# Eight consecutive rows of wo per partition, heads re-sorted by 0/1 products, and another order of the tail in a two-problem decode attention

## The chip, the cores and the metric

The kernel runs on one core of a Trainium2 chip. The metric is the time of one execution in microseconds on the device. Three executions of the kernel before took 377.95, 378.59 and 376.51 us (median 377.95). A fourth was recorded by the hardware profiler.

The core has a matrix engine (PE: a weight load followed by a matmul that streams up to 512 columns), a vector engine (DVE), a scalar engine (ACT), GpSimd (POOL), and SP, which here only issues transfers. Matmuls write to PSUM, the engines read from it, and transfers go between HBM and SBUF by 16 DMA engines. The engines run side by side and wait for one another through semaphores.

## The reference

Two independent problems A and B of the same shape, each one decode step with a sliding window; the outputs stand side by side.

```python
B, Sq, D = 2, 1, 576
Hq, Hkv, Sk, Dh = 32, 16, 16384, 128
W = min(4096, max(256, Sk // 4))                     # 4096
q = (x @ wq).reshape(B, Sq, Hq, Dh)                  # transposed to b h q d
k = repeat(k_cache[:, :, Sk - W:, :], 2, axis=1)     # 2 query heads share a kv head
v = repeat(v_cache[:, :, Sk - W:, :], 2, axis=1)
p = softmax(einsum("bhqd,bhkd->bhqk", q, k) * Dh ** -0.5)
o = einsum("bhqk,bhkd->bhqd", p, v)
out = o.reshape(B, Sq, Hq * Dh) @ wo                 # wo: [4096, 576]
```

Everything is bf16. For each of 2 x 32 pairs (problem, kv head, batch) a K slab and a V slab of 4096 x 128 elements, 1 MiB each, are read once. With wq and wo this makes 153 MB.

## The kernel before

**Units.** A *pair* i (0 to 63) is one kv head of one batch of one problem: 32 in A, then 32 in B. Two pairs in a row (both batches of one kv head) are a *norm unit* k = 0 to 31. Eight pairs are a *group* G = 0 to 7; a group covers four kv heads, so eight query heads, and has its own softmax and its own slice of wo (8 x 128 rows of 576 elements).

**Steps.** The body is a loop over time steps t, each with four quarters q. In step t DVE transposes the K slab of pair t (four STREAM_TRANSPOSE, L679), PE computes the scores of pair t - 1 (eight matmuls, L700) into one PSUM bank per group, and PE multiplies the V slab of pair t - LAG with the softmax weights, LAG = 11. Work that belongs between these is hung into tables by (step, quarter): `pe_pre` and `da_pre` ahead of the quarter's work, `da_post` behind it. Every operation is recorded with the operations it needs, and each engine runs its own list in the order of recording, waiting on semaphores.

**Softmax of a group.** After the last scores of group G (step T = 8G + 8) DVE takes the maximum (`c_max`, L377, in `da_post`), PE turns it (L381), DVE negates and copies it (L391, L401), PE spreads it (L406), ACT takes the exponential (L427) and DVE transposes the weights into `pT` (L473) and gathers them into `pC` (L487). The sums go by L431, L441, L448 and L451 into `rsb` (L463), in step T + 2.

**Values, two forms.** `is_a(i)` says which form a pair takes; the last NB_TAIL = 7 pairs are not `is_a`.
- `is_a`: eight matmuls with the small weights `pC` stationary and 512 columns of V moving (L765) into an accumulator bank `ACC[i % 2]`; eviction to `acc_sb[i % 2]` by ACT for even i (L780) and by DVE for odd i (L783); then, one step later, four matmuls with the identity (L743) combine the parts into the bank `OT[k % 2]`. In a step the combination of the pair before stands directly ahead of the product of the pair at hand.
- otherwise: 32 matmuls with V stationary and 56 columns of `pT` moving (L723), eight in each quarter, straight into `OT[k % 2]`. The last V slab arrives in four transfers, one per quarter.

**Norm and projection.** In step tn_of(k) DVE multiplies a unit's output by `rsb` (`make_norm`, L555, result `oTn`: 128 positions of a head in the partitions, two heads, two batches), clears the `OT` bank again (L565), and one quarter later PE multiplies it with its two heads of wo (`make_proj`, four matmuls of 2 x 288, L582) and adds it to columns 128 to 415 of both `OT` banks. At the end of each problem `make_E` copies these to `out_sb` (L597, L600), and two transfers write it out.

**Transfers.** SP issues all loads in one list. `stream` alternates K of pair t and V of pair t - LAG; they share a ring of NR = 9 slabs, and a slab's transfer waits until the slab nine places before it has been read. The wq chunks and the wo slices stand in the list ahead of given K slabs; the wo slice of group G stands ahead of K of pair 8G + 6, has two buffers `wob[:, G % 2]`, and waits for the last projection of group G - 2 (`deps` in `issue_wo`). SP works strictly in order: what stands behind a waiting transfer waits too.

The wo slice is read so that partition d holds row d of each of its eight heads: 1024 runs of 576 elements, 1,152 bytes.

Of the kernel before, what the change touches and what calls it, by code (L numbers as in the profile page):

```python
# [6 lines left out]
BF16 = mybir.dt.bfloat16  # L7
ACTF = mybir.ActivationFunctionType
# [51 lines left out]
def build_kernel(nc, probs, out, cfg=None):  # L60
# [6 lines left out]
    LAG = cfg.get("LAG", 11)  # L67
    NPT = 3
    NS = cfg.get("NS", 56)
    NB_TAIL = cfg.get("NB_TAIL", 7)  # L70
    WQ_AT = cfg.get("WQ_AT", 13)
    QP_AT = cfg.get("QP_AT", 21)
    WO_LEAD = cfg.get("WO_LEAD", 5)
# [37 lines left out]
    def pair_info(i):  # L111
# [3 lines left out]
        b = il % Bb  # L115
        return P, g, b

    def tile_cols(j):
        return (j % 16) * 32 + 16 * (j // 16)

    es = ExitStack()
    with es:
# [25 lines left out]
        rs = sb("rs", [1, 16], FP32)  # L148
        rsb = sb("rsb", [128, NPT, 16], FP32)
        oTn = sb("oTn", [128, 2, 2, Bb], BF16)  # L150
        acc_sb = sb("acc_sb", [8, 2, 512], BF16)
        pC = sb("pC", [128, NPT, 2, 8, 32], BF16)
        out_sb = sb("out_sb", [Bb, NPROB, NOUT], BF16)
# [131 lines left out]
        def issue_wo(G):  # L285
            P = G // GPP
            Gl = G % GPP
            woP = probs[P][4]
            h0 = Gl * 8
            pc = G % 2  # L290
            deps = [proj[4 * (G - 2) + 3]] if G >= 2 else []

            def f(e):
                return e.dma_start(wob[:, pc, :, :],
                                   woP[h0 * 128:(h0 + 8) * 128, :].rearrange("(h d) n -> d h n", d=128)).then_inc(wo_sem[pc], 16)
            wo_dma[G] = dma_op("sp", wo_sem[pc], 1, f, deps, "wo%d" % G)

        def ensure_stream_until(s_needed):
# [73 lines left out]
        def c_max(G):  # L372
            x = G % 2
            deps = [Sop[(8 * G + 7, NQ - 1)]]
            if G >= 1:
                deps.append(chain[(G - 1, "Tm")])
            chain[(G, "max")] = S.add("dve", lambda e: e.tensor_reduce(m1[:], ST[x][:, :], AX.X, ALU.max),  # L377
                                      deps, "cmax_%d" % G)
# [168 lines left out]
        def make_norm(k):  # L547
            x = k % 2
            G = (2 * k) // 8
            gl = k % 4  # L550
            pr = G % NPT
            orr = k % 2

            def f(e):
                return e.tensor_tensor(oTn[:, orr, :, :].rearrange("d h b -> d b h"),  # L555
                                       OT[x][:, 0:64 * Bb].rearrange("d (b c) -> d b c", b=Bb, c=64)[:, :, 0:2],
                                       rsb[:, pr, gl * 2 * Bb:(gl + 1) * 2 * Bb].rearrange("d (b h) -> d b h", b=Bb, h=2),
                                       ALU.mult)
            deps = [PVop[(2 * k + 1, NQ - 1)], chain[(G, "rsb")], ot_last_pe[x]]
            if k >= 2:  # L560
                deps.append(proj[k - 2])
            op = S.add("dve", f, deps, "norm_%d" % k)
            norm_mul[k] = op
            if k + 2 < NK:
                ot_zero[k + 2] = S.add("dve", lambda e: e.memset(OT[x][:, 0:64 * Bb], 0.0), [op], "otz_%d" % (k + 2))  # L565
            else:
                ot_zero[k + 2] = op
            ot_last_da[x] = ot_zero[k + 2]

        def make_proj(k):  # L570
# [17 lines left out]
            ot_last_pe[0] = proj[k]  # L588
            ot_last_pe[1] = proj[k]

        def make_E(P, which, final):
            k_last = (P + 1) * KP - 1
            deps = [proj[k_last], ot_last_pe[which]]
            if which == 0:
                if not final:
                    deps.append(norm_mul[k_last + 1])
                op = S.add("dve", lambda e: e.tensor_copy(out_sb[:, P, 0:NH], OT[0][0:Bb, ACC0:ACC0 + NH]),  # L597
                           deps, "Elo_%d" % P)
# [14 lines left out]
        def at(tbl, t, q, fn):  # L613
            tbl.setdefault((t, q), []).append(fn)

        da_post = {}
        for G in range(NG):
            T = 8 * G + 8
            at(da_post, T, 3, lambda G=G: c_max(G))
            at(pe_pre, T + 1, 0, lambda G=G: c_tm(G))  # L620
            at(da_pre, T + 1, 0, lambda G=G: c_nm(G))
            at(pe_pre, T + 1, 2, lambda G=G: c_bias(G))
            at(da_pre, T + 1, 2, lambda G=G: (c_exp(G), c_tpx(G)))
            at(da_pre, T + 1, 3, lambda G=G: c_gather(G))
            at(pe_pre, T + 2, 0, lambda G=G: c_ts(G))
            at(da_pre, T + 2, 0, lambda G=G: c_rs(G))
            if G + 2 < NG:
                at(da_pre, T + 2, 0, lambda G=G: make_st_zero(G + 2))
            at(pe_pre, T + 2, 1, lambda G=G: c_rsbm(G))
            at(da_pre, T + 2, 1, lambda G=G: c_rsb(G))  # L630
            P, Gl = G // GPP, G % GPP
            at(pe_pre, 2 * Gl if P == 0 else QP_AT + 8 * GPP * (P - 1) + Gl, 2 if G > 0 else 0, lambda G=G: make_qproj(G))
            at(pe_pre, max(0, 8 * G - 3), 2 if G > 0 else 0, lambda G=G: make_qjob(G))
        def tn_of(k):
            return (2 * k + 1) + LAG + (2 if is_a(2 * k + 1) else 1)
        for k in range(NK):
            tn = tn_of(k)
            at(da_pre, tn, 0, lambda k=k: make_norm(k))
            at(pe_pre, tn, 1, lambda k=k: make_proj(k))
        for P in range(NPROB):  # L640
            final = (P == NPROB - 1)
            k_last = (P + 1) * KP - 1
            tp_ = tn_of(k_last)
            if final:
                at(da_pre, tp_, 2, lambda P=P: (make_E(P, 0, True), make_E(P, 1, True)))
            else:
                at(da_pre, tp_, 2, lambda P=P: make_E(P, 1, False))
                assert tn_of(k_last + 1) > tp_
                at(da_pre, tn_of(k_last + 1), 0.5, lambda P=P: make_E(P, 0, False))

        def make_late_zero():
# [6 lines left out]
            ot_last_da[0] = init_zero["OT0"]  # L658
            ot_last_da[1] = init_zero["OT1"]
        at(da_pre, 1, 0, make_late_zero)  # L660

        NT = NP + LAG + 3
        for t in range(NT):
            for q in range(NQ):
# [21 lines left out]
                if 0 <= i < NP:  # L686
                    G = group_of(i)
                    x = G % 2
                    c = i % NKT
                    pl = i % 8  # L690
                    zr = G % NZQ

                    def fS(e, x=x, c=c, pl=pl, zr=zr, q=q):
                        last = None
                        jh = q // 2
                        for p4 in (2 * (q % 2), 2 * (q % 2) + 1):
                            b32, par = p4 // 2, p4 % 2
                            b0 = xt[:, c, 2048 * jh + 64 * b32 + par:2048 * jh + 64 * b32 + par + 1]
                            mv = bass.AP(b0.tensor, b0.offset, [list(b0.ap[0]), [128, 16], [2, 32]])
                            last = e.matmul(ST[x][:, 0:512], zq[:, p4, zr, pl, 16 - 16 * jh:144 - 16 * jh], mv,  # L700
                                            start=False, stop=True, skip_group_check=True)
                        return last
                    jh_ = q // 2
                    deps = [EVop[(i, 2 * jh_)], EVop[(i, 2 * jh_ + 1)], qev[G], st_zero[G]]
                    Sop[(i, q)] = S.add("pe", fS, deps, "S_%d_%d" % (i, q))
                i = t - LAG
                if 0 <= i < NP and not is_a(i):
                    sV = slab_idx[("V", i)]
# [180 lines left out]
```

## Time and profile before

| | |
|---|---|
| median of three executions (range) | 377.95 us (376.51 to 378.59) |
| the profiled execution: its time, its span | 378.42 us, 376.6 us |
| PE busy, DVE busy, ACT busy | 296.3 us (79%), 211.7 us (56%), 36.9 us (10%) |
| bytes moved, mean rate over the span | 153.41 MB, 407 GB/s |
| DMA packets, of them under 2 KB | 28661, 10592 |
| mean granted PE clock | 0.964 of full speed |
| L700 scores, one matmul of 512 columns | 391 ns, x512 |
| L765 values, one matmul of 512 columns | 397 ns, x456 |
| L582 projection, one matmul of 288 columns | 285 ns, x128 |
| L783, L780 eviction (DVE, ACT) | 679 ns, 586 ns |

The span runs from the first to the last instruction; the profiled execution's own time is 1.8 us more. The duration of one matmul contains its way through the array, which neighbours share: eight L765 matmuls in a row take 1.83 us and not eight times 397 ns. "Idle before" an instruction is put down to what ended it. The chain that ended last goes back from the last instruction to whatever released each one; a line of it gives its start, its length and what ran. In the stretches, a line gives the stretch, its length, the busy time of PE, of the weight loads, of DVE, ACT and POOL (with counts), the granted PE clock, the DMA engines' share and GB/s.

### The profile page before, as it was taken

Reading aid. Unit: us, or ns where it says so; the run is one execution under the profiler, and the core shown is the slowest. Engines: PE = TensorE matmul, PEld = TensorE weight load, DVE = VectorE, ACT = ScalarE, POOL = GpSimd, SP = SyncE. Lnnn points to the kernel's source line nnn. Section 1 sums busy time; section 2 is a strip of 40 time slices with the busy share of each in tenths; the row PEclk is TensorE's granted clock in tenths of the full one; section 3 lists DMA queues with packets and bytes.
Section 4 is the critical chain, followed back from the end, with each engine's and each line's share of the span. In section 5 each row is a group of like instructions: output and inputs, shape, how many; then the busy total and the mean of one; then the engine's idle time right before and its main releaser. Section 6 shows DMA issues by size and latency. Waiting matters only on the chain.

```text
span 376.6 us, 4709 instructions
## 1 busy us (share of the span) xinstructions
PE 296.3 (79%) x1960; PEld 118.6 (31%) x1960; DVE 211.7 (56%) x429; ACT 36.9 (10%) x105; POOL 6.7 (2%) x22
## 2 busy tenths in 40 slices
PE   0397778375898989969897789868799689959786
PEld 0243223122334433313332233323333233313245
DVE  3196894235664567626864567636773467633311
ACT  1101101000101010100101010100101001000100
POOL 7000000000000000000000000000000000000000
PEclk9999989799999999989999899999999899998899
DMA  8999999999999999999999999999999999999991
GB/s 310 425 421 412 419 419 411 422 420 422 422 416 417 418 420 420 410 421 421 423 419 411 422 419 422 410 422 421 422 422 410 420 425 419 413 421 418 425 411 70
DMA packets 28661, 153.41 MB, mean 407 GB/s; under 512 B 2392, under 2 KB 10592, under 8 KB 11360
## 3 DMA queue, kind: packets, MB, share of 16 engines
q1 hardware_dynamic: 28632, 153.11, 98.9%
q8 instruction: 15, 0.25, 0.3%
q14 instruction: 6, 0.05, 0.0%
q10 hardware_dynamic: 8, 0.00, 0.0%
HBM read 153.10 MB, written 0.00 MB: 407 GB/s over the span
## 4 chain that ended last, share of the span: by engine, by line
DMA 44%; PE 33%; DVE 10%; SPq 9%; issue 1%; ACT 1%
DMA ring<-in_B_v_cache_dram 17%; DMA ring<-in_A_v_cache_dram 15%; PE acc L765 15%; PE st L700 11%; DMA ring<-in_A_k_cache_dram 8%; SPq L272 7%; DMA ring<-in_B_k_cache_dram 5%; DVE xt L679 4%; PE ot L582 3%; DVE acc_sb L783 2%; PE ot L723 2%; PE ot L743 1%; ACT pR L427 1%; DVE m L377 1%; DVE pT L473 1%
## 5 line engine op out<-in xcount | busy, mean ns | idle before, releaser
L679 DVE STREAM_TRANSPOSE xt<-ring 128x512 f32<-128x512 f32 x256 | 159.3, 673 | 66.0 <-DMA ring<-in_A_k_cache_dram 38.5
L765 PE MATMUL acc<-ring,pC 128*8 128x512 bf16 x456 | 114.7, 397 | 38.1 <-DMA ring<-in_A_v_cache_dram 22.9
L700 PE MATMUL st<-xt,zq 128*128 128x512 bf16 x512 | 134.7, 391 | 4.9 <-DVE xt L679 4.5
L700 PEld LDWEIGHTS st<-xt,zq 128*128 128x128 bf16 x512 | 42.7, 98 | 74.1 <-issue 28.5
L765 PEld LDWEIGHTS acc<-ring,pC 128*8 128x8 bf16 x456 | 36.0, 89 | 91.1 <-DMA ring<-in_A_v_cache_dram 24.5
L783 DVE CAST acc_sb<-acc 8x512 bf16<-8x512 f32 x28 | 19.0, 679 | 66.8 <-PE acc L765 66.8
L780 ACT ACTIVATE acc_sb<-acc 8x512 bf16<-8x512 f32 x29 | 17.0, 586 | 186.1 <-PE acc L765 186.1
L582 PE MATMUL ot<-wob,oTn 128*2 128x288 bf16 x128 | 20.8, 285 | 3.5 <-DVE ot L565 3.2
L743 PEld LDWEIGHTS ot<-ident_b,acc_sb 8*128 8x128 bf16 x228 | 9.2, 92 | 24.1 <-issue 16.1
L743 PE MATMUL ot<-ident_b,acc_sb 8*128 8x56 bf16 x228 | 15.6, 185 | 0.8 <-DVE acc_sb L783 0.8
L509 PE MATMUL tb<-xT,wqb 128*128 128x56 bf16 x256 | 10.2, 192 | 6.4 <-DMA wqr<-in_A_wq_dram 6.4
L582 PEld LDWEIGHTS ot<-wob,oTn 128*2 128x2 bf16 x128 | 8.0, 82 | 15.5 <-issue 8.1
L509 PEld LDWEIGHTS tb<-xT,wqb 128*128 128x128 bf16 x256 | 9.8, 99 | 7.9 <-DMA wqr<-in_A_wq_dram 6.5
L381 PE MATMUL tb<-ident_f,m 128*1 128x128 f32 x8 | 2.2, 270 | 11.7 <-DVE m L377 11.7
L555 DVE TENSOR_TENSOR oTn<-ot,rsb 128x4 bf16<-128x4 f32 x32 | 4.1, 127 | 11.2 <-PE ot L723 7.4
L541 ACT ACTIVATE zq<-tb 32x64 bf16<-32x64 f32 x32 | 7.1, 221 | 31.9 <-PE tb L523 31.6
L509 PE MATMUL tb<-xT,wqr 128*128 128x56 bf16 x64 | 9.5, 192 | 0.0
L473 DVE STREAM_TRANSPOSE pT<-pR 128x512 bf16<-128x512 bf16 x8 | 5.7, 711 | 4.6 <-ACT pR L427 4.6
L419 ACT ACTIVATE bias_sb<-tb 128x1 f32<-128x1 f32 x8 | 1.4, 171 | 61.0 <-PE tb L406 61.0
L723 PE MATMUL ot<-pT,ring 128*128 128x56 bf16 x224 | 7.0, 187 | 0.4 <-issue 0.4
L723 PEld LDWEIGHTS ot<-pT,ring 128*128 128x128 bf16 x224 | 6.2, 96 | 2.0 <-issue 1.9
L565 DVE MEMSET ot<- 128x128 f32 x30 | 5.0, 165 | 3.1
(50 smaller groups left out, 71.9 us busy)
## 6 DMA issues: line engine op xcount, KB each, us to landing
ring<-in_A_k_cache_dram SPq DMA_DIRECT2D x32, 1024.0 KB, 20.2
ring<-in_A_v_cache_dram SPq DMA_DIRECT2D x32, 1024.0 KB, 19.8
ring<-in_B_k_cache_dram SPq DMA_DIRECT2D x32, 1024.0 KB, 20.3
ring<-in_B_v_cache_dram SPq DMA_DIRECT2D x31, 1024.0 KB, 19.3
wob<-in_A_wo_dram SPq DMA_DIRECT2D x4, 1152.0 KB, 18.4
wob<-in_B_wo_dram SPq DMA_DIRECT2D x4, 1152.0 KB, 9.5
wqb<-in_A_wq_dram SPq DMA_DIRECT2D x4, 1024.0 KB, 8.0
wqb<-in_B_wq_dram SPq DMA_DIRECT2D x4, 1024.0 KB, 21.9
```

The source lines that it names most:

```text
L272: return e.dma_start(ring[:, r, :], src).then_inc(ring_sem[r], 16)
L473: chain[(G, "pT")] = S.add("dve", lambda e: e.transpose(pT[:, pr, 0:PW], pR[:, G % 2, :]), deps, "cTpx_%d" % G)
L509: last = e.matmul(bank[:, hl * 64:hl * 64 + NS], w_, x_, start=(ch == 0), stop=(ch == NCH - 1))
L541: last = e.activation(dst, src, ACTF.Copy)
L582: last = e.matmul(OT[half][0:Bb, ACC0:ACC0 + NH], oTn[:, orr, h, :], wob[:, pc, hsl + h, half * NH:(half + 1) * NH], start=False, stop=Tru ...
L679: xop = S.add("dve", lambda e, r=r, c=c, q=q: e.transpose(xt[:, c, q * 1024:(q + 1) * 1024].bitcast(FP32), ring[:, r, q * 1024:(q + 1) * 1 ...
L700: last = e.matmul(ST[x][:, 0:512], zq[:, p4, zr, pl, 16 - 16 * jh:144 - 16 * jh], mv, start=False, stop=True, skip_group_check=True)
L723: last = e.matmul(OT[x][:, b * 64:b * 64 + NS], ring[:, r, j * 128:(j + 1) * 128], pT[:, pr, col:col + NS], start=False, stop=True, skip_g ...
L743: last = e.matmul(OT[x][:, b * 64:b * 64 + NS], acc_sb[0:8, i % 2, 128 * jl4:128 * jl4 + 128], ident_b[0:8, 2 * jl4:2 * jl4 + NS], start=F ...
L765: last = e.matmul(ACC[i % 2][0:8, 0:512], pC[:, pr, jh, pl, 8 * cb:8 * cb + 8], ring[:, r, j0_ * 128:(j0_ + 4) * 128], start=(n_ == 0), st ...
L780: ev_ = S.add("act", lambda e, i=i: e.activation(acc_sb[0:8, i % 2, :], ACC[i % 2][0:8, :], ACTF.Copy), d, "accev_%d" % i)
L783: ev_ = S.add("dve", lambda e, i=i: e.tensor_copy(acc_sb[0:8, i % 2, :], ACC[i % 2][0:8, :]), d, "accev_%d" % i)
```

## The change

For groups 0 to 6 (`by_group`) the wo slice is read as eight *consecutive* rows per partition: partition p holds rows 8p to 8p + 7, so 128 runs of 9,216 bytes. Row 8p + s of the slice belongs to head p // 16 and position 8 (p % 16) + s, so the heads' outputs have to be brought into that order. The norms of the group's four units write into `oTg` (128 positions, 8 heads, 2 batches). When the last is done, DVE multiplies it by a 0/1 mask into `om` (`make_spread`: 128 partitions x 128 elements), PE multiplies it in eight matmuls of 16 columns with shifted 0/1 matrices (`make_redist`), ACT copies the result to `Rsb` (`make_rev`), and PE makes the group's 16 projection matmuls in one piece (`make_gproj`), all in the step of the group's last norm, in its quarters 0 to 3. Group 7 keeps the old reading and its projections by unit. Three DVE instructions in step 3 make the 0/1 matrices (`make_sel`).

In the tail: NB_TAIL goes from 7 to 4, so pairs 57 to 59 take the L765 form; group 7's `c_max` is recorded right after the last scores instead of after the step's V work (`da_mid`), its sums are taken in step T + 4 instead of T + 2, and the projection of unit 30 comes one step later. The first problem's `make_E` moves from quarter 2 of its step to the start of the next one.

The wait of a wo slice on the projections of group G - 2 is now one on the group's single projection piece.

```diff
-    NB_TAIL = cfg.get("NB_TAIL", 7)
+    NB_TAIL = cfg.get("NB_TAIL", 4)
...
+    def by_group(G):
+        return G < NG - 1
...
-                return e.dma_start(wob[:, pc, :, :],
-                                   woP[h0 * 128:(h0 + 8) * 128, :].rearrange("(h d) n -> d h n", d=128)).then_inc(wo_sem[pc], 16)
+                rows = woP[h0 * 128:(h0 + 8) * 128, :]
+                src = rows.rearrange("(p s) n -> p s n", s=8) if by_group(G) else rows.rearrange("(h d) n -> d h n", d=128)
+                return e.dma_start(wob[:, pc, :, :], src).then_inc(wo_sem[pc], 16)
...
+            dst = oTg[:, G % 2, 2 * gl:2 * gl + 2, :] if by_group(G) else oTn[:, orr, :, :]
...
+        def make_spread(G):
+            deps = [norm_mul[4 * G + j] for j in range(4)] + [init_zero["maskS"]]
+            if G >= 2:
+                deps.append(redist[G - 2])
+            spread[G] = S.add("dve", lambda e: e.tensor_tensor(
+                om[:, G % 2, :, :, :],
+                oTg[:, G % 2, :, :].unsqueeze(2).broadcast_to([128, 8, 8, Bb]),
+                maskS[:].unsqueeze(1).unsqueeze(3).broadcast_to([128, 8, 8, Bb]), ALU.mult), deps, "spread_%d" % G)
+
+        def make_redist(G):
+            def fn(e, bank):
+                last = None
+                for hl in range(8):
+                    last = e.matmul(bank[:, 0:8 * Bb], selL[:, 112 - 16 * hl:240 - 16 * hl],
+                                    om[:, G % 2, hl, :, :].rearrange("d s b -> d (s b)"), start=(hl == 0), stop=(hl == 7))
+                return last
+            n, bank, op = tb_job(fn, "redist_%d" % G, [spread[G], init_zero["selL"]])
...
+            r_ev[G] = S.add("act", lambda e: e.activation(Rsb[:, G % 2, :, :].rearrange("d s b -> d (s b)"),
+                                                          bank[:, 0:8 * Bb], ACTF.Copy), deps, "rev_%d" % G)
...
+        def make_gproj(G):
+            P = G // GPP
+            k = 4 * G + 3
+
+            def f(e):
+                last = None
+                for s_ in range(8):
+                    for half in range(2):
+                        last = e.matmul(OT[half][0:Bb, ACC0:ACC0 + NH], Rsb[:, G % 2, s_, :],
+                                        wob[:, G % 2, s_, half * NH:(half + 1) * NH],
+                                        start=False, stop=True, skip_group_check=True)
+                return last
+            deps = [r_ev[G], wo_dma[G], acc_zero[P][0], acc_zero[P][1], ot_last_da[0], ot_last_da[1]]
+            proj[k] = S.add("pe", f, deps, "gproj_%d" % G)
...
-            at(da_post, T, 3, lambda G=G: c_max(G))
+            tail = G == NG - 1
+            at(da_mid if tail else da_post, T, 3, lambda G=G: c_max(G))
...
-            at(pe_pre, T + 2, 0, lambda G=G: c_ts(G))
-            at(da_pre, T + 2, 0, lambda G=G: c_rs(G))
+            Ts = T + 4 if tail else T + 2
+            at(pe_pre, Ts, 0, lambda G=G: c_ts(G))
+            at(da_pre, Ts, 0, lambda G=G: c_rs(G))
...
-            at(pe_pre, tn, 1, lambda k=k: make_proj(k))
+            if by_group(G):
+                if k % 4 == 3:
+                    at(da_pre, tn, 0, lambda G=G: make_spread(G))
+                    at(pe_pre, tn, 1, lambda G=G: make_redist(G))
+                    at(da_pre, tn, 2, lambda G=G: make_rev(G))
+                    at(pe_pre, tn, 3, lambda G=G: make_gproj(G))
+            elif k == NK - 2:
+                at(pe_pre, tn + 1, 1, lambda k=k: make_proj(k))
+            else:
+                at(pe_pre, tn, 1, lambda k=k: make_proj(k))
...
-                at(da_pre, tp_, 2, lambda P=P: make_E(P, 1, False))
+                at(da_pre, tp_ + 1, 0, lambda P=P: make_E(P, 1, False))
...
+        at(da_pre, 3, 0, make_sel)
```

More of the change, by code (lines that the diff above doesn't have):

```diff
@@ L150, in build_kernel @@
         oTn = sb("oTn", [128, 2, 2, Bb], BF16)
+        oTg = sb("oTg", [128, 2, 8, Bb], BF16)
+        om = sb("om", [128, 2, 8, 8, Bb], BF16)
+        Rsb = sb("Rsb", [128, 2, 8, Bb], BF16)
+        maskS = sb("maskS", [128, 8], BF16)
+        selL = sb("selL", [128, 240], BF16)
         acc_sb = sb("acc_sb", [8, 2, 512], BF16)
@@ L552, in make_norm @@
             orr = k % 2
+            dst = oTg[:, G % 2, 2 * gl:2 * gl + 2, :] if by_group(G) else oTn[:, orr, :, :]
             def f(e):
-                return e.tensor_tensor(oTn[:, orr, :, :].rearrange("d h b -> d b h"),
+                return e.tensor_tensor(dst.rearrange("d h b -> d b h"),
                                        OT[x][:, 0:64 * Bb].rearrange("d (b c) -> d b c", b=Bb, c=64)[:, :, 0:2],
@@ L559, in make_norm @@
             deps = [PVop[(2 * k + 1, NQ - 1)], chain[(G, "rsb")], ot_last_pe[x]]
-            if k >= 2:
+            if by_group(G):
+                if G >= 2:
+                    deps.append(spread[G - 2])
+            elif (k - 2) in proj and not by_group((2 * (k - 2)) // 8):
                 deps.append(proj[k - 2])
@@ L589, in make_proj, with make_sel @@
             ot_last_pe[1] = proj[k]
+        spread = {}
+        redist = {}
+        redist_n = {}
+        r_ev = {}
+        def make_sel():
+            S.add("dve", lambda e: e.memset(selL[:], 0.0), [], "zero_selL")
+            z = S.ops["dve"][-1]
+            a_ = S.add("dve", lambda e: e.tensor_reduce(selL[:, 112:128], ident_b[:, 0:128].rearrange("d (a s) -> d a s", s=8),
+                                                        AX.X, ALU.max), [z, p_ident_b], "selL")
+            b_ = S.add("dve", lambda e: e.tensor_reduce(maskS[:], ident_b[:, 0:128].rearrange("d (a s) -> d s a", s=8),
+                                                        AX.X, ALU.max), [p_ident_b], "maskS")
+            init_zero["selL"] = a_
+            init_zero["maskS"] = b_
@@ new lines, in make_spread @@
+        def make_spread(G):
+            deps = [norm_mul[4 * G + j] for j in range(4)] + [init_zero["maskS"]]
+            if G >= 2:
+                deps.append(redist[G - 2])
[11 more added lines that the diff above has]
+            n, bank, op = tb_job(fn, "redist_%d" % G, [spread[G], init_zero["selL"]])
+            redist[G] = op
+            redist_n[G] = (n, bank)
@@ new lines, in make_rev @@
+        def make_rev(G):
+            n, bank = redist_n[G]
+            deps = [redist[G]]
+            if G >= 2:
+                deps.append(proj[4 * (G - 2) + 3])
+            r_ev[G] = S.add("act", lambda e: e.activation(Rsb[:, G % 2, :, :].rearrange("d s b -> d (s b)"),
+                                                          bank[:, 0:8 * Bb], ACTF.Copy), deps, "rev_%d" % G)
+            tb_consumer[n] = r_ev[G]
+        def make_gproj(G):
[11 more added lines that the diff above has]
+            proj[k] = S.add("pe", f, deps, "gproj_%d" % G)
+            ot_last_pe[0] = proj[k]
+            ot_last_pe[1] = proj[k]
@@ L616, in build_kernel @@
         da_post = {}
+        da_mid = {}
         for G in range(NG):
             T = 8 * G + 8
-            at(da_post, T, 3, lambda G=G: c_max(G))
+            tail = G == NG - 1
+            at(da_mid if tail else da_post, T, 3, lambda G=G: c_max(G))
             at(pe_pre, T + 1, 0, lambda G=G: c_tm(G))
@@ L624, in build_kernel @@
             at(da_pre, T + 1, 3, lambda G=G: c_gather(G))
-            at(pe_pre, T + 2, 0, lambda G=G: c_ts(G))
-            at(da_pre, T + 2, 0, lambda G=G: c_rs(G))
+            Ts = T + 4 if tail else T + 2
+            at(pe_pre, Ts, 0, lambda G=G: c_ts(G))
+            at(da_pre, Ts, 0, lambda G=G: c_rs(G))
             if G + 2 < NG:
                 at(da_pre, T + 2, 0, lambda G=G: make_st_zero(G + 2))
-            at(pe_pre, T + 2, 1, lambda G=G: c_rsbm(G))
-            at(da_pre, T + 2, 1, lambda G=G: c_rsb(G))
+            at(pe_pre, Ts, 1, lambda G=G: c_rsbm(G))
+            at(da_pre, Ts, 1, lambda G=G: c_rsb(G))
             P, Gl = G // GPP, G % GPP
@@ L637, in build_kernel @@
             tn = tn_of(k)
+            G = (2 * k) // 8
             at(da_pre, tn, 0, lambda k=k: make_norm(k))
-            at(pe_pre, tn, 1, lambda k=k: make_proj(k))
+            if by_group(G):
+                if k % 4 == 3:
[7 more added lines that the diff above has]
+                at(pe_pre, tn, 1, lambda k=k: make_proj(k))
         for P in range(NPROB):
@@ L705, in build_kernel @@
                     Sop[(i, q)] = S.add("pe", fS, deps, "S_%d_%d" % (i, q))
+                for fn in da_mid.get((t, q), []):
+                    fn()
                 i = t - LAG
```

## The prediction

> **What bounds the kernel now.** I read the page's slices first, for the stage in which each resource is full.
>
> ```profile
> DMA  8999999999999999999999999999999999999991
> GB/s 310 425 421 412 419 419 411 422 420 422 422 416 417 418 420 420 410 421 421 423 419 411 422 419 422 410 422 421 422 422 410 420 425 419 413 421 418 425 411 70
> ```
>
> From the second slice to the last but one the DMA engines never rest, and the rate stays at 410 to 425 GB/s. In the body of the span only fewer bytes or cheaper bytes help. The last slice is another stage: 70 GB/s, so the transfers end about 5 us ahead of the span's end (the last quarter of the last V slab, pair 63, reports its landing at 371.60). The dips to 410 stand where a wo slice passes, which I made sure of with stretches of 12 us, with and without one:
>
> ```profile
> 194.00:206.00 12.00, 10.98 (x63) 4.11 (x62) 5.36 (x11) 1.74 (x6) 0.00 (x0) 1.00 1.03 413
> 238.00:250.00 12.00, 10.26 (x58) 3.77 (x58) 6.15 (x14) 1.87 (x6) 0.00 (x0) 1.00 1.03 414
> 257.00:269.00 12.00, 9.32 (x49) 3.52 (x50) 6.99 (x15) 1.53 (x4) 0.00 (x0) 1.00 1.02 423
> 300.00:312.00 12.00, 10.63 (x59) 4.03 (x58) 8.48 (x17) 1.53 (x4) 0.00 (x0) 1.00 1.01 422
> ```
>
> The last column is GB/s: 413 or 414 with a wo slice, 422 or 423 without. Then the chain of work that ended last, in order of time, for the end:
>
> ```profile
> 326.85 11.65 DMA ring<-in_B_v_cache_dram
> ...
> 338.54 2.40 PE acc L765 x8
> ...
> 344.11 1.82 PE acc L765 x8
> ...
> 348.67 1.83 PE acc L765 x8
> ...
> 350.52 0.68 DVE acc_sb L783
> 351.20 0.61 DVE m L377
> ...
> 353.25 3.29 PE acc L765 x8
> ...
> 358.67 1.83 PE acc L765 x8
> ...
> 360.52 0.69 DVE acc_sb L783
> ...
> 361.26 0.27 PE ot L743 x4
> 361.53 1.82 PE acc L765 x8
> ...
> 366.35 1.57 PE ot L723 x56
> ...
> 374.58 0.45 DVE out_sb L597
> ```
>
> The last DMA in the chain is V of pair 51, landed at 338.5. Behind it all is PE, with DVE between: the products of pairs 52 to 56 (L765), then the seven direct ones (L723). PE is late, not the data: V of pair 56 had landed at 353.4 and is multiplied at 361.5. So the tail, 38 us long, is bound by PE's order, and there the two forms differ greatly. A pair in the L765 form goes PV, eviction, combination, and without S products in between PE waits for the eviction: 358.67 to 361.53 is 2.86 us a pair. In the L723 form 56 products take 1.57, so 32 take 0.90.
>
> **The change, part by part.** All against the profiled execution (378.42 us, span 376.6, so 1.8 outside; it is 0.47 above the median).
>
> *Seven wo slices in runs of 9,216 bytes instead of 1,152.* By the stretches a slice costs 12 x (422 - 413) / 422 = 0.26 us more than its bytes at a slab's rate. By the landings (last of the 16 engines) a slice takes 3.00 where its 1.125 slabs at 2.48 would take 2.79: 0.21. Seven times: 1.5 to 1.8; nothing, if long runs went no faster. I take 1.5. The end moves with it, as the tail's chain hangs on a landing. The Trainium skill, "DMA: Bandwidth & Descriptors", Specifications, gives 512 bytes as the least transfer for line rate: by that, both forms are at line rate, this term is 0 and the sum below would be 381.7. The dips speak against it.
>
> *Norm, spread, redistribution, projection by group.* Per group PE gets 8 redistributions (L723's row, 0.028 each: about 0.4 us; with 16 columns hardly more), ACT one more copy of 128x16 (L463's row, 183 ns), DVE one spread of 128 elements (between L555's 127 ns and L487's 252: 0.2). The 16 projections stay 16, now in one piece: four take 0.58, so 2.3. Some 0.4 us more PE per group in a body where PE is busy 79% and waits for slabs: hidden by the DMA, and 7 x (0.4 + 0.2 + 0.2) = 5.6 if that cover were gone. The three DVE instructions that make the 0/1 matrices (each under L377's 0.67) stand in step 3, where DVE waits for K slabs (38.5 us in all): nothing; 1.5 uncovered. The evictions of the first problem's outputs move half a step: nothing waits for them before the next group's projection.
>
> *The wait in front of wo on SP.* SP issues wo of group G only when the projections of G - 2 are done, and the K and V slabs behind it queue up:
>
> ```profile
> SPq L294 <- PE ot L582: 62.0, 6, 10.9
> ```
>
> Six waits, 62.0 us. The group's projection now ends later in its step: 0.4 for redistribution, four S products (0.9), and 2.3 instead of 0.6, so +3.0; less a projection removed in the step before last (0.6): 2.4. What is left in the DMA queues decides. wo's first packets start 4.3, 3.0, 3.3, 2.9, 2.2 and 2.8 us after the issue, and about 1.0 of that is the way (first issue at 0.80, first packet at 1.83): the engine that is ahead has 1.2 to 3.3 us left, the one that is behind 2.0 to 3.6 more (spread of the 16 landings). So the leading engines run dry for up to 1.2 us, the last one, which sets each landing, does not. Taken: 0; the bound above is rival 5. SP's issue of the K slab behind wo (2.70 us at 324.11, 0.43 elsewhere) may shorten with fewer runs; it is hidden either way.
>
> *The tail.* Pairs 57 to 59 go from L723's form to L765's, projections 24 to 27 leave their places, the maximum goes ahead of pair 53's product, the sums move to two steps later. I walk PE's order from the start of pair 53's product, before at 348.67 (27.9 to the end). After, that start comes 1.5 earlier by DMA and 0.58 by the projection gone between S products: 346.6. Then, each PV 1.83:
> - 53 to 54: eviction 0.70, then -max, its copy and the bias product; the maximum (0.61) now lies beside PV: 3.6 (before 4.6).
> - 54 to 55: PV, ACT's eviction 0.65, combination 0.27: 2.8. Before 5.4, of which 1.46 was half clock (3.29 for 1.83) and the rest the sums and a projection.
> - 55 to 56: 2.9, as before.
> - 56 to 57: PV 1.8; sums to the broadcast 0.95; norm, memset, spread 0.6; redistribution 0.4; ACT's copy 0.25; projections 2.3; combination 0.2: 6.5.
> - 57 to 58 and 58 to 59: 2.9 + 2.8 (projection 28 fits into an eviction).
> - from 59 to the end: PV 1.8, 32 direct 0.9, combination 0.2, 8 direct and norm 0.75, projection 0.65, 64 direct 1.85, projection 0.6, 24 direct 0.85, norm 0.25, projection 0.65, output 0.5, its DMA 1.5: 10.5, less 0.2 of overlaps: 10.3.
>
> Sum 31.8, so the end is at 378.4 (+1.8), 380.2 us with what lies around it. V of pair 63 lands near 370 and waits.
>
> **The half clock** is the term that could come back. Stretches of 3.41 us, the width of the profile's own half-clock records:
>
> ```profile
> 350.02:353.43 3.41, 1.42 (x12) 0.59 (x10) 1.77 (x4) 0.23 (x2) 0.00 (x0) 1.00 1.01 420
> 353.43:356.84 3.41, 3.41 (x9) 0.78 (x7) 1.12 (x3) 0.97 (x3) 0.00 (x0) 0.50 1.01 423
> ```
>
> PE was busy 42% of the first (the chain through the maximum), and the next was granted 0.50. In my walk the idle pieces are 1.0 and 0.7 us, so no stretch falls so low; I leave the 1.5 out. The Trainium skill, "TensorE: Matmul & The Clock Gate", Part 1, says that the clock falls after at least one idle window of about 3.4 us; this trace is stricter, as a window 42% busy was enough. By the page no part of the new tail is slowed (380.2); by the row, one unlucky window gives 381.7.
>
> **The rivals.**
> 1. *The end still goes by the DMA.* If the combinations found their evictions done, the end would be V 63's landing 371.60 - 1.5, plus 8 products and the output path: 0.4 + 2.95 (373.65 to 376.6), so 373.5 and 375.3 us, faster. It decides from a step of about 2.0 us a pair in place of 2.8. For it: there are two accumulators and two copies. Against: in PE's built order each combination stands directly behind the product of its own pair, and 360.52/361.26 shows the wait.
> 2. *Part of the lengthening*: the engines' lags fall otherwise (an instruction load of 16 KB holds one DMA engine for 1.1 us, and the page counts 15) and one eviction is hidden: 380.2 - 1.1 - 0.7 = 378.4, no change by the bound.
> 3. *One half-clock stretch in the tail*: 380.2 + 1.5 = 381.7.
> 4. *wo is no faster, the change not doing what it says*: 380.2 + 1.5 = 381.7. Against: the dips.
> 5. *SP's wait empties all queues.* If the leading engines set the pace, 1.2 us in each of six places: +7, 387. For it: margins of 1.2 at the least. Against: landings follow the last engine.
>
> **How the numbers follow.** What a measurement of this kernel can tell from no change is about 0.5%: 376.1 to 379.8. Forecast 0.58 (own range 378.9 to 381.7; 0.41 of it above 379.8, 0.17 within); rival 1 0.13; 2 0.08; 3 0.09; 4 0.06; 5 0.06. Faster 0.13; within 0.17 + 0.08 = 0.25; slower 0.41 + 0.21 = 0.62. The range of 8 in 10 leaves out rivals 1 and 5 (0.19): from 377.0, which is rival 2 with two more evictions of 0.7 hidden, to 383.2, which is rivals 3 and 4 together.
>
> **What would show it.** Right: the slices lose their dips to 410 but for the last; the last landing near 370 and the end 8 us behind it; pairs 54 to 59 in the L765 form 2.8 apart, with one gap of 6.5; SP's wait for wo up by some 14 us with the rate unbroken. Wrong: a last landing past 371 (no shorter transfers, or dry queues, then seen as slices under 400); PE waiting for V in the last 10 us (rival 1); 0.50 records past 345 (rival 3).

## The result, and the profile after

The changed kernel takes 380.12 us (median of 19, 379.08 to 384.70), the kernel before in the same comparison 377.90 us. The ratio is 1.007, 95% interval 1.0046 to 1.0095: slower by 0.7%. The interval lies clear of 1, and its lower end is just under the 0.5% that the prediction took for the least difference that can be told. The profiled execution took 380.92 us, its span is 379.1.

The slices of the page for the kernel after, DMA share and rate:

```profile
DMA  7999999999999999999999999999999999999980
GB/s 314 425 421 421 420 420 425 419 422 419 422 390 418 424 418 422 420 422 422 423 419 421 423 418 424 415 425 418 425 415 424 418 423 421 399 428 418 424 340 2
```

The dips to 410 at the wo slices are gone, as the prediction had it. Two new dips stand there: 390 in the twelfth slice, where SP issues wo of group 2 (at 111.84), and 399 in the thirty-fifth, where wo of group 7 passes, which keeps its short runs. Slices under 400 were one of the prediction's signs of being wrong; more of them under *SP's wait* below. And the last slice moves 2 GB/s instead of 70: the transfers end earlier, the kernel later. The same stretches of 12 us as before (the last column is GB/s):

```profile
194.00:206.00 12.00, 10.98 (x68) 4.56 (x66) 5.33 (x11) 1.47 (x5) 0.00 (x0) 1.00 1.01 423
238.00:250.00 12.00, 9.79 (x60) 3.91 (x58) 5.95 (x14) 1.87 (x6) 0.00 (x0) 1.00 1.01 419
```

413 and 414 have become 423 and 419. By the landings a wo slice in long runs takes 2.78 to 2.80 us in five of the seven groups, not 3.00; groups 2 and 3 took 2.89 and 3.11 in this execution. In kernel 1 below all seven take 2.78 to 2.80. The last landing is at 369.84 instead of 371.60.

The end of the chain of work that ended last, in order of time (start, length, what):

```profile
325.45 11.99 DMA ring<-in_B_v_cache_dram
...
337.49 3.58 PE acc L856 x8
341.06 2.84 PE st L789 x8
...
347.98 1.83 PE acc L856 x8
...
351.52 1.83 PE acc L856 x8
...
354.29 1.83 PE acc L856 x8
356.13 0.02 issue
356.15 0.69 DVE acc_sb L874
...
357.16 1.82 PE acc L856 x8
...
360.93 2.12 PE ot L657 x16
...
363.26 1.83 PE acc L856 x8
...
366.13 1.83 PE acc L856 x8
...
368.90 1.82 PE acc L856 x8
...
375.37 0.74 PE ot L814 x24
...
377.04 0.45 DVE out_sb L672
```

L856 is what L765 was, L789 was L700, L814 was L723, L874 was L783. The last DMA in the chain is again V of pair 51, landed at 337.44; behind it all is PE, with the evictions and the small work of DVE and ACT between. The products of pairs 53 to 59 follow one another at 3.54, 2.77, 2.87, 6.10, 2.87 and 2.77 us, each with an eviction between, and the last three quarters of pair 63, landed by 369.84, are multiplied at 375.37.

SP's waits, and the stretches of 3.41 us around the start of the tail:

```profile
SPq L304 <- PE ot L657: 73.5, 6, 12.4
```

```profile
332.83:336.24 3.41, 0.65 (x7) 0.16 (x4) 1.28 (x3) 0.00 (x0) 0.00 (x0) 1.00 1.01 425
336.24:339.65 3.41, 2.16 (x6) 0.69 (x7) 1.21 (x3) 0.00 (x0) 0.00 (x0) 0.50 1.01 423
339.65:343.06 3.41, 3.41 (x9) 0.90 (x8) 1.96 (x4) 0.00 (x0) 0.00 (x0) 0.50 1.01 423
```

Six waits of 73.5 us in all for wo, 11.5 more than before. PE was busy 19% of the first stretch, waiting for V of pair 51, and the next two were granted half the clock. Behind 343.06 no record at half clock stands in the span.

### The profile page after: what moved, and what is told of

It is laid out like the page before. It is cut to its first block, busy times and chain, and to the rows that moved or that the text cites. A ratio compares the mean times of both kernels' runs of the same rounds, so it can differ in the third digit from the quotient of the medians.

```text
span 379.1 us, 4722 instructions
## 1 busy us (share of the span) xinstructions
PE 300.4 (79%) x1956; PEld 123.2 (33%) x1956; DVE 215.0 (57%) x441; ACT 38.7 (10%) x113; POOL 6.7 (2%) x22
## 4 chain that ended last, share of the span: by engine, by line
DMA 56%; PE 31%; DVE 7%; SPq 4%; issue 1%; ACT 1%
DMA ring<-in_A_v_cache_dram 24%; DMA ring<-in_B_v_cache_dram 24%; PE acc L856 15%; PE st L789 8%; DMA ring<-in_A_k_cache_dram 8%; DVE xt L768 4%; PE ot L657 4%; SPq L280 2%; DVE acc_sb L874 2%; SPq L304 1%; PE ot L834 1%; PE ot L814 1%; PE tb L518 1%; SPq L289 1%; PE ot L596 1%
## 5 line engine op out<-in xcount | busy, mean ns | idle before, releaser
L856 PE MATMUL acc<-ring,pC 128*8 128x512 bf16 x480 | 121.9, 400 | 39.3 <-DMA ring<-in_A_v_cache_dram 23.3
L789 PE MATMUL st<-xt,zq 128*128 128x512 bf16 x512 | 135.2, 395 | 4.5 <-DVE xt L768 4.2
L856 PEld LDWEIGHTS acc<-ring,pC 128*8 128x8 bf16 x480 | 38.1, 89 | 95.4 <-DMA ring<-in_A_v_cache_dram 24.6
L789 PEld LDWEIGHTS st<-xt,zq 128*128 128x128 bf16 x512 | 43.8, 99 | 72.0 <-issue 24.9
L874 DVE CAST acc_sb<-acc 8x512 bf16<-8x512 f32 x30 | 20.4, 679 | 74.2 <-PE acc L856 74.2
L518 PE MATMUL tb<-xT,wqb 128*128 128x56 bf16 x256 | 10.2, 192 | 6.3 <-DMA wqr<-in_A_wq_dram 6.3
L657 PE MATMUL ot<-wob,Rsb 128*2 128x288 bf16 x112 | 14.8, 286 | 0.3 <-ACT Rsb L645 0.3
L657 PEld LDWEIGHTS ot<-wob,Rsb 128*2 128x2 bf16 x112 | 8.8, 83 | 6.7 <-issue 2.6
L386 DVE TENSOR_REDUCE m<-st 128x1 f32<-128x512 f32 x8 | 5.4, 670 | 3.2 <-PE st L789 3.2
L518 PEld LDWEIGHTS tb<-xT,wqr 128*128 128x128 bf16 x64 | 6.3, 99 | 0.0
```

Source lines behind the costliest of these rows:

```text
L518: last = e.matmul(bank[:, hl * 64:hl * 64 + NS], w_, x_, start=(ch == 0), stop=(ch == NCH - 1))
L657: last = e.matmul(OT[half][0:Bb, ACC0:ACC0 + NH], Rsb[:, G % 2, s_, :], wob[:, G % 2, s_, half * NH:(half + 1) * NH], start=False, stop=Tr ...
L856: last = e.matmul(ACC[i % 2][0:8, 0:512], pC[:, pr, jh, pl, 8 * cb:8 * cb + 8], ring[:, r, j0_ * 128:(j0_ + 4) * 128], start=(n_ == 0), st ...
L874: ev_ = S.add("dve", lambda e, i=i: e.tensor_copy(acc_sb[0:8, i % 2, :], ACC[i % 2][0:8, :]), d, "accev_%d" % i)
```

## The experiments

Each kernel was timed in turns with the kernel before, whose times gather at three levels: in one set of 29 executions 14 lie at 376.4 to 376.8, 4 at 377.8 to 378.0 and 11 at 378.7 to 379.3, so its median came out at 376.65 in one comparison and at 377.86 or 377.90 in the others. Differences to that median can therefore be off by a microsecond; the ratios, which are to the kernel before, are not taken from it. Where two of the kernels below are compared, their own medians are.

**1. Seven direct pairs again.** The changed kernel with one number put back:

```diff
-    NB_TAIL = cfg.get("NB_TAIL", 4)
+    NB_TAIL = cfg.get("NB_TAIL", 7)
```

> The changed kernel with one number put back: the last 7 pairs, not 4, take the direct form. Theory (the tail is bound by PE's order; three more pairs in the L765 form cost it): from pair 53's product to the end 3.5 + 2.8 + 2.9 + 6.6 + 11.4 = 27.2 us instead of 31.1, span about 375.2, time about 377.0, so 3 to 4 us less than the changed kernel and up to 1 us less than the kernel before. Rival (the tail is neutral, the body pays for the group-wise projection and the longer wait of SP): 380 to 381, like the changed kernel.

Measured: 375.04 us (374.69 to 376.00), ratio 0.9942 (0.9918 to 0.9967). Faster than both, 5.1 us less than the changed kernel and 2 us better than the theory's own walk. The end of its chain:

```profile
366.93 2.59 PE ot L814 x96
369.51 0.58 PE ot L596 x4
370.09 0.74 PE ot L814 x24
...
371.76 0.45 DVE out_sb L672
```

The last landing was at 369.62: PE arrives at pair 63's last three quarters (370.09) half a microsecond later. The tail is now balanced against the transfers. The rival, a cost in the body, is out: the body is the same in both.

**2. The tail's order alone**, with the old reading of wo everywhere:

```diff
     def by_group(G):
-        return G < NG - 1
+        return False
```

> The changed kernel with the old reading of wo and the old projections in all groups, so only the order of the tail is changed. Theory: no 1.5 us from the DMA, but also no 6.1 us gap at pairs 56 to 57 (about 3.9, with one projection there): 379 to 380.5, 0.3 to 0.7% slower than before. Rival (the cost lies in the body's new work): 377.5 to 378.5, like before.

Measured: 379.65 us (379.18 to 380.94), ratio 1.0061 (1.0037 to 1.0084), as the theory had it. The slowdown needs nothing of the re-sorting. From pair 56 to 57, with one projection between:

```profile
359.56 1.82 PE acc L856 x8
...
363.40 1.83 PE acc L856 x8
```

**3. The re-sorting alone**, with the tail of before:

```diff
-    NB_TAIL = cfg.get("NB_TAIL", 4)
+    NB_TAIL = cfg.get("NB_TAIL", 7)
...
-            tail = G == NG - 1
+            tail = False
...
-            elif k == NK - 2:
-                at(pe_pre, tn + 1, 1, lambda k=k: make_proj(k))
```

> The changed kernel with the tail of before (7 direct pairs, maximum behind the step's V work, sums two steps after the group, unit 30 projected in its own step); only the rows of wo, the re-sorting and the projection by group are left of the change. Theory: last landing about 1.5 earlier than before, near 370, and a tail of about 28 us, in which group 6's projection in one piece takes back some 2 us: 376.5 to 378. Rival (the body pays): 379.5 to 381, and the DMA rate broken at the wo slices.

Measured: 378.53 us (375.33 to 379.20), ratio 1.0018 (0.9993 to 1.0042): no difference that this shows, half a microsecond above the theory's range, and scattered over 4 us. In the profiled execution (span 375.9) the wo slice of group 7 took 3.81 us by the landings instead of the 2.96 it has before; the DMA share was 0.92 and 0.91 in the two microseconds from 327 to 329, so some queues did run dry there. In the chain, pair 54's product runs at half clock as before (3.49 us), and group 6's projection in one piece (2.05 us) stands in PE's order. The gain of the rows does not show in this order of the tail.

**4. Four direct pairs in the kernel before.**

```diff
-    NB_TAIL = cfg.get("NB_TAIL", 7)
+    NB_TAIL = cfg.get("NB_TAIL", 4)
```

> The kernel before with one number changed: 4 direct pairs instead of 7. Theory: three pairs at 2.8 us instead of 0.9 each, less what projections fill of the evictions' waits: 4 to 5.5 us slower than before, 381.5 to 383.5. Rival (the end hangs on the last landing at 371.6): within 0.5 us of before, since the landing does not move.

Measured: 381.35 us (379.78 to 383.06), ratio 1.0103 (1.0064 to 1.0142): 3.9 us by the ratio, just under the theory's range and far from the rival. The chain, at the three pairs that changed form:

```profile
361.46 1.83 PE acc L765 x8
...
364.23 1.83 PE acc L765 x8
366.06 0.02 issue
366.09 0.69 DVE acc_sb L783
...
367.10 1.83 PE acc L765 x8
...
369.87 1.82 PE acc L765 x8
371.69 0.93 PE ot L723 x32
```

Starts 2.8 to 2.9 apart, the direct pair 0.93. The last landing, at 370.83, is if anything earlier than before, so the end does not hang on it.

**5. Three wo buffers**, on top of 1, so that SP's wait for wo is over long before:

```diff
-        wob = sb("wob", [128, 2, 8, NOUT], BF16)
+        wob = sb("wob", [128, 3, 8, NOUT], BF16)
...
-            deps = [proj[4 * (G - 2) + 3]] if G >= 2 else []
+            deps = [proj[4 * (G - 3) + 3]] if G >= 3 else []
```

(and three semaphores, and G % 3 in place of G % 2 for the buffer)

> The changed kernel with 7 direct pairs and three wo buffers instead of two, so that SP's wait in front of a wo slice is on the projections of group G - 3 and is over long before. Theory (the wait costs nothing, the last DMA engine never runs dry): within 0.4 us of the same kernel with two buffers (375.0), all wo slices 2.78 to 2.80 in the steps of landings. Rival (the wait lets DMA engines run dry and the transfers end later): 0.7 to 2 us less, 373 to 374.3, and the last landing earlier by as much.

Measured: 375.06 us (374.97 to 375.48), ratio 0.9925 (0.9896 to 0.9954): the same as 1. What changed is the spread of the 16 engines at the last landing: 365.81 to 370.00, where kernel 1 has 367.03 to 369.62. Without the wait the leading engines run 1.2 us further ahead, the last one does not finish earlier. So in kernel 1 SP's wait costs nothing in the median: the engines that it makes idle are ahead.

**6. Ten direct pairs.**

```diff
-    NB_TAIL = cfg.get("NB_TAIL", 4)
+    NB_TAIL = cfg.get("NB_TAIL", 10)
```

> The changed kernel with 10 direct pairs: pairs 54 to 56 also take the direct form. Theory (with 7 the end already hangs on the last landing, so nothing more is to be had from PE): 374.3 to 375.5, within 0.7 us of 375.0, and PE waits for V at the end. Rival (PE's order still sets the end): three steps shorter by 1.9 each, so several us less, limited by the landing at 369.6 plus 3.4 us: 373.0 span, 374.8. What tells them apart is the chain: DMA in its last 10 us, or PE throughout.

Measured: 376.16 us (374.72 to 378.31), ratio 0.9965 (0.9938 to 0.9992). Nothing more to be had, as the theory said, but the median is 0.7 above its range. The chain has a DMA in its last 10 us, and the stretches of 3.41 us behind show what PE did:

```profile
350.28 18.98 DMA ring<-in_B_v_cache_dram
```

```profile
362.99:366.41 3.42, 1.69 (x36) 1.20 (x36) 0.19 (x2) 0.00 (x0) 0.00 (x0) 1.00 1.01 414
366.41:369.82 3.41, 2.19 (x44) 2.05 (x45) 0.16 (x1) 0.00 (x0) 0.00 (x0) 0.50 0.93 352
369.82:373.23 3.41, 3.41 (x57) 2.62 (x55) 0.00 (x0) 0.00 (x0) 0.00 (x0) 0.50 0.10 38
```

PE now waits for V, is busy half of a stretch (1.69 of 3.42), and the last products run at half clock: the cheaper work makes itself dearer. In this execution the wo slice of group 5, issued at 241.16, also took 4.52 us by the landings (the last landing is at 371.79), and there the queues ran dry:

```profile
241.00:242.00 1.00, 1.00 (x9) 0.37 (x8) 0.00 (x0) 0.40 (x1) 0.00 (x0) 1.00 0.33 123
```

SP had waited 12.2 us there for the group's projection two groups earlier, so this is the wait in front of wo, and it made the slice 1.7 us longer in this execution. What it and the half clock each add to the median cannot be told apart.

**7. The maximum late**, on top of 1:

```diff
-            at(da_mid if tail else da_post, T, 3, lambda G=G: c_max(G))
+            at(da_post, T, 3, lambda G=G: c_max(G))
```

> The changed kernel with 7 direct pairs and the last group's maximum put back behind the step's V work. Theory: the way from pair 53's product to 54's goes from 3.5 back to 4.6, and PE's idle share there brings back a half-clock stretch of 3.41 us (1.5 us): 376 to 377.5, 1.0 to 2.5 more than 375.0. Rival (the maximum's place is hidden behind the landing): within 0.4 us of 375.0.

Measured: 378.54 us (376.98 to 382.92), ratio 1.0021 (0.9990 to 1.0052): 3.5 us more than kernel 1 and a microsecond beyond the theory's range; without the longest execution the median is 378.06, 3.0 more and half a microsecond beyond. The rival is out. The chain:

```profile
346.29 1.83 PE acc L856 x8
...
350.88 3.45 PE acc L856 x8
```

4.59 us from pair 53 to 54, as in the kernel before, and then pair 54 at half clock (3.45 for 1.83). The profiled execution is 377.2 us, among the faster of its twelve. Of the slower ones only the clock is known: the four shortest executions were granted 0.950 on average, the eight others 0.938.

**8. The sums early**, on top of 1:

```diff
-            Ts = T + 4 if tail else T + 2
+            Ts = T + 2
```

> The changed kernel with 7 direct pairs and the last group's sums put back to two steps after the group. Theory: 0.7 us more between pairs 54 and 55, about 1 us less at group 6's projection, where norm and spread can then go on beside a product: 374.4 to 375.2, no change against 375.0. Rival (the later sums are what made the tail short): 376 to 377.

Measured: 375.60 us (374.75 to 378.34), ratio 0.9944 (0.9919 to 0.9970). 0.6 more than kernel 1, with intervals that overlap, and between the ranges of theory and rival. In its profiled execution (376.86 us) the wo slice of group 7 took 3.81 us and the last landing came at 371.73, 2.1 later than in kernel 1, and the end hangs on it; that alone can explain this execution, without the sums. The place of the sums is worth little, and whether anything is open.

**9. Matmuls into the idle time before V of pair 51**, in the changed kernel; their result is read by nobody:

```diff
+        def make_warm():
+            def fn(e, bank):
+                last = None
+                for _ in range(14):
+                    last = e.matmul(bank[:, 0:512], ident_b[:, 0:128], wqb[:, 0, 0:512], start=True, stop=True)
+                return last
+            n, bank, op = tb_job(fn, "warm", [p_ident_b, wq_dma[(1, 0)]])
+            tb_consumer[n] = op
+        at(pe_pre, 62, 3, make_warm)
```

> The changed kernel (4 direct pairs) with 14 matmuls of 512 columns, whose result nobody reads, where PE idles 4.0 us before V of pair 51 lands; at full clock they take 3.0. Theory (that idle time is what puts pair 51's and 52's work at half clock, and PE's order then carries the loss to the end): no half-clock record between 336 and 344, pair 51's product 1.8 instead of 3.6 and the scores behind it 1.9 instead of 2.8, the end 2 to 2.7 earlier, 377.4 to 378.2. Rival (the half clock comes by itself, or the loss is absorbed later): 379.8 to 381.

Measured: 379.94 us (378.54 to 380.49), ratio 1.0058 (1.0037 to 1.0079): a miss in time. It lies in the rival's range and is not to be told from the changed kernel's 1.007. The profiled execution (378.74 us) does show the clock that was expected:

```profile
326.57 15.29 DMA ring<-in_B_v_cache_dram
...
341.90 1.89 PE acc L866 x8
343.79 1.85 PE st L799 x8
```

No half-clock record between 299 and 376, and pair 52's product starts when its data land (341.86) instead of at 344.11. That is 2.2 us less than the changed kernel's profiled execution, but that one was itself 0.8 above its median, and the nine times here stand in two groups, four at 378.5 to 378.9 and five at 379.9 to 380.5; the second is not explained. So the half clock ahead of the tail is shown for the profiled execution, and what it costs in the median is not.

**10. The same matmuls in kernel 1.**

> The changed kernel with 7 direct pairs and the same 14 matmuls. Theory (the end is then close to the last landing, 369.6 plus 3.4 us of output path): at most 0.8 less than 375.0, 374.2 to 375.0. Rival (PE's order still sets the end there too): 2 to 2.7 less, 372.4 to 373.

Measured: 376.06 us (374.75 to 378.31), ratio 0.9960 (0.9940 to 0.9980): no gain, rather 1 us more than kernel 1, scattered, and outside both ranges. In its profiled execution the last landing is at 370.53, 0.9 later than in kernel 1. What makes it later is open.

**11. Kernel 1 with the old rows** (`by_group` as in 2, seven direct pairs):

> The changed kernel with 7 direct pairs and with the old reading of wo and the old projections in all groups: the order of the tail without the re-sorting. Theory (the rows are worth their 1.5 us of DMA where the end hangs on the last landing): last landing at 371 to 371.6, 376.0 to 377.0, 1 to 2 us more than 375.0. Rival (the rows' gain is taken back by the projection in one piece): 374.7 to 375.5, the same.

Measured: 376.58 us (376.41 to 376.77), ratio 0.9973 (0.9958 to 0.9988). Its chain:

```profile
354.95 16.35 DMA ring<-in_B_v_cache_dram
371.30 0.05 issue
371.35 0.40 PE ot L814 x8
...
372.65 0.02 issue
372.67 0.45 DVE out_sb L672
```

Here the end does hang on the last landing: PE takes eight products 0.05 us after it. The twelve times lie within 0.4 us, at the lowest of the three levels of the kernel before. Against kernel 1 the old rows cost 376.58 - 375.04 = 1.54 us, and the ranges of the two do not touch.

## Why the prediction was right, step by step

| step | predicted | measured |
|---|---|---|
| one wo slice in long runs | 0.21 less | 3.00 to 2.79: 0.21 in five groups; 2.89 and 3.11 in two |
| seven of them, at the last landing | 1.5 | 371.60 to 369.84: 1.8 |
| SP's wait for wo, six places | +14 | 62.0 to 73.5: +11.5 |
| start of pair 53's product | 346.6 | 347.98 |
| 53-54, 54-55, 55-56 | 3.6, 2.8, 2.9 | 3.54, 2.77, 2.87 |
| 56-57, with the projection piece | 6.5 | 6.10 |
| 57-58, 58-59 | 2.9, 2.8 | 2.87, 2.77 |
| from pair 59 to the end | 10.3 | 10.2 |
| end of the span | 378.4 | 379.1 |
| time | 380.2 | 380.12 median, 380.92 profiled |

*What sets the end.* The prediction said PE's order and not the data. Kernels 1, 2 and 4 show it from three sides: the number of direct pairs alone, 4 instead of 7, adds 4.7 us in the kernel before (376.65 to 381.35; 3.9 by the ratio), 3.1 with the new order of the tail and the old rows (376.58 to 379.65, kernels 11 and 2) and 5.1 with the new rows (375.04 to 380.12). The last landing of the profiled executions hardly moves in each of these pairs: 371.60 and 370.83, 371.30 and 371.36, 369.62 and 369.84.

*The rows.* Worth what was computed where the landing counts: 1.54 us from kernel 11, whose end hangs on it, to kernel 1, where PE arrives 0.47 behind it. With the tail of before they bring nothing that shows (kernel 3), and neither do they with four direct pairs: 379.65 without and 380.12 with them, which the intervals do not separate. There the last group's projection in one piece stands in PE's order, 6.10 us from pair 56 to 57 instead of 3.84 in kernel 2, and its 2.3 us more take the place of the 1.5 saved.

*The other edits of the tail* pull the other way: with the old rows and seven direct pairs the ratio is 0.9973 (kernel 11), 1.0 us less than the kernel before. Kernel 7 shows that the place of the maximum is the large one among them; the later projection of unit 30 was not tried alone.

*The half clock.* The step that failed is the start of the tail. The walk let the start come 1.5 earlier; the landing of V of pair 51 came 1.05 earlier, and the two stretches at half clock took that back: pair 51's product and the scores behind it took 3.58 + 2.84 = 6.4 us, where the kernel before had 2.40 + 2.96 = 5.4. Its lines, with the two stretches around them:

```profile
338.54 2.40 PE acc L765 x8
340.94 2.96 PE st L700 x8
```

```profile
336.37:339.78 3.41, 1.24 (x6) 0.53 (x7) 2.14 (x4) 0.00 (x0) 0.00 (x0) 1.00 1.01 423
339.78:343.19 3.41, 3.41 (x10) 0.98 (x8) 2.22 (x4) 0.00 (x0) 0.00 (x0) 0.50 1.02 420
```

So the kernel before loses clock here too, for one stretch; the changed kernel waits longer and loses two. With 0.69 for the projection gone, 348.67 becomes 347.98. The prediction had looked for idle time inside the new tail, found none, and was right there (350.00 to 353.40: 2.32 us busy, clock 1.00); it left out the 4.0 us of waiting just ahead of it. That V came 1.05 and not 1.5 earlier belongs to this execution: in kernel 1 it landed at 336.66, 1.8 earlier than in the kernel before, and was met by two stretches at half clock as well (335.78 to 342.61). The walk from there was 0.7 too long, so the profiled end is 0.7 late, and that the median meets the forecast within 0.1 is in part luck.

The Trainium skill, "TensorE: Matmul & The Clock Gate", Part 1, has the clock fall after an idle window of about 3.4 us. The trace agrees as to the width (its records are 3.413 us or multiples, up to the one that the end cuts off), not as to how idle: 19% busy was enough here, 42% in the kernel before, and half in kernel 6.

*SP's wait.* Taken as 0, and in the median it is (kernel 5). In single executions it is not always: in the profiled one of the changed kernel some queues ran dry at group 2's slice,

```profile
111.00:114.00 3.00, 3.00 (x21) 1.22 (x18) 0.00 (x0) 0.00 (x0) 0.00 (x0) 1.00 0.86 318
```

share 0.86 and 318 GB/s. The 16 landings of that wo slice lie 0.8 us apart, those of the slab ahead of it 1.7: the leaders had waited. The last engine lost 0.1 us by it. At group 7's slice the share was 0.94 from 326 to 328, and the slab that lands just ahead of that slice took 3.27 us instead of 2.48; whether the wait did this or another lag of one engine is open. By the last landing, 369.84 against 369.62 in kernel 1, most of that was made up. So the prediction's sign for its last rival, slices under 400, did appear, with a small part of its cost. Elsewhere it was more: single wo slices in the profiled executions of kernels 3 and 8 (3.81, group 7, else 2.96) and 6 (4.52, group 5, else 2.79) took 0.9 and 1.7 longer.

## What to carry to other kernels

A kernel that moves data at a steady rate for 95% of its span can still be decided in its last 10%: find the last DMA in the chain, and walk what stands behind it by the starts of neighbouring instructions, not by their durations. Two forms of the same product can be worth different things in the body and in the tail, where no other work fills the wait for an eviction any more (2.8 us a pair against 0.9 here); choose the number of tail units so that the compute arrives with the last landing, no earlier (in kernel 6 PE then idles, and its last products run at half clock) and no later. And a gain in bytes shows in the time only when the end hangs on a landing: the same rows were worth 1.5 us in one order of the tail and nothing that shows in two others.

## What the hardware showed beyond that

- The 13 traces of this case, cut along the grid of the clock's own records (3.41 us), show when the clock falls. Each of the 76 stretches at full clock in which PE was busy under 40% was followed by one at half clock; of the 58 between 40% and 55%, 24 were; of the more than 1,000 above 55%, none. From half clock it came back after none of the 39 stretches that were busy under 75%.
- The levels of the kernel before go with the clock: in the set of 29 executions the mean granted clock is 0.957 at the lowest level, 0.946 at the middle one and 0.942 at the highest, over 2.9 us in time. Kernel 11, whose end hangs on a landing, has clocks from 0.936 to 0.977 and no levels at all (0.4 us over twelve executions).
- The 16 DMA engines do not keep together: by the last landing the leader is 2.4 to 4.2 us ahead of the last. What made the leaders wait cost nothing as long as the last one did not wait too (kernel 5 against 1).
- In the kernel before, from group 2 on, one of the three transfers that SP issues behind a wo slice took 1.8 to 3.3 us to issue each time (2.70 us at 324.11); behind the slices in 128 runs of the changed kernel, groups 2 to 6, none took more than 0.45 but one (1.26). It is not the number of runs alone: behind group 7's slice, which keeps its 1,024 runs there, the longest of these issues is 0.66. As SP's time was hidden, this brought nothing.
